# Which row tile's statistics run on ScalarE at the head of an attention kernel

## The chip, the cores and the metric

The kernel runs on one core of one Trainium2 chip. The metric is the device time of one execution in microseconds; lower is better. The kernel before took 1938.25 us, the median of three runs (1937.86 to 1939.1).

## The reference, cut to what matters

A layer norm of x (2048 rows of 640) feeds an attention with 32 heads of width 192 over a cached K and V, and a gated feed-forward of width 1536. The two results are multiplied and added to x. All is in bfloat16.

```python
def reference(A_x, A_k_cache, A_v_cache, A_wq, A_wo, B_x, B_w1, B_w3, B_w2):
    ...
    x = A_x
    xn = _layernorm(x, axis=-1)          # (x - m) / sqrt(v + 1e-5)
    s = _A_ref(xn, A_k_cache, A_v_cache, A_wq, A_wo)
    g = _silu(_B_ref(xn, B_w1, B_w3, B_w2))
    return x + s * g
```

## The kernel before

PE's score and value products make up some 70% of the chain of work that ended last, and PE's other products nearly all of the rest. The change is in what comes first: the layer norm of the first 512 rows (four tiles of 128), which must be ready before PE can turn (transpose) and project them. This beginning of the kernel is called its head below; an attention head is named as such. There are two ways to get a tile's statistics, one on VectorE and one on ScalarE:

```python
    def ln_stats(g, i):                       # VectorE
        ...
        for a in range(nsub):
            nc.vector.bn_stats(out=stats[:, a, :], in_=xr[:, a, :])
        nc.vector.bn_aggr(out=mv[:, i, :], in_=stats[:])
        if i % 2 == 1:                        # the pair is complete: add eps, take the power
            nc.vector.tensor_scalar(out=ve[:, i - 1:i + 1, 0], in0=mv[:, i - 1:i + 1, 1], scalar1=eps, ...)
            ln_rstd(g, i)                     # GpSimd: rstd = ve ** -0.5, for both tiles of the pair

    def ln_stats_act(g, i):                   # ScalarE: mean, then sum of squares about it
        ...
        nc.scalar.activation(out=xns[g, i][:], in_=xi, func=ACT.Identity, scale=1.0 / D, accum_out=mv[:, i, 0:1])
        nc.scalar.activation(out=xns[g, i][:], in_=xi, func=ACT.Square, scale=-1.0, bias=mv[:, i, 0:1], accum_out=ss[:])
        lnorm["ss"] = ss
```

The head then runs:

```python
    def head_start():
        load_x(0, 0, 2)                       # tiles 0 and 1 of x
        load_x(0, 2, 4)                       # tiles 2 and 3
        load_k0(0, nc.sync)
        load_w0()
        turn_over(44)                         # PE: 44 products to keep it busy
        ln_stats(0, 0)
        ln_stats(0, 1)
        ln_stats_act(0, 3)
        load_k0(1, nc.scalar)                 # second half of the first K head
        load_x(1, queue=nc.scalar)
        load_v(0, (0,), nc.scalar)
        ln_stats(0, 2)
        ... # adds of tiles 2 and 3
        ln_rstd(0, 3)
        load_w(1)
        for i in range(4):
            ln_norm(0, i, nc.vector)
        ...
        ln_turn(0, 0, nc.scalar.copy)         # PE transposes of tiles 0 and 1
        turn_k0(pk0, 0, range(4))             # PE transposes of the first half of K
        ln_turn(0, 1, nc.vector.tensor_copy)
        turn_k0(pk1, 1, (0, 1))
        swap_halves(0)                        # DMA: copy with partitions 0-63 and 64-127 exchanged
        ...
        load_v(0, (1,))
        load_x(2)                             # same queue, behind the swap
        project_first()
        ...
        ln_turn_dma(1, 0)                     # transposing loads of the second block's tiles,
        ln_turn_dma(1, 1)                     # same queue, behind load_x(2)
```

After it comes the stream of heads, blocks of 512 rows and pairs of key tiles. Two of its steps: `project(1, 0)`, the first projection that reads the swapped copy (`xnS`), and `project0(1)`, which needs the tiles that `ln_turn_dma` turned.

```python
        if h == 0 and qb == 0 and p == 3:
            project(1, 0)
        if h == 0 and qb + 1 < NQB and p == (5 if qb == 0 else 4):
            project0(qb + 1)
```

Of the kernel before, what the change touches and what calls it, by code (L numbers as in the profile page):

```python
# [9 lines left out]
ALU = mybir.AluOpType  # L10
# [118 lines left out]
def _kernel_impl(  # L129
# [12 lines left out]
    nc = tc.nc  # L142
    _, SQ, D = A_x.shape
    _, H, SK, dh = A_k_cache.shape
# [15 lines left out]
    eps = 1e-5  # L160
# [52 lines left out]
    def load_x(g, t0=0, t1=4, queue=nc.sync):  # L213
        queue.dma_start(out=x_sb[:, 4 * g + t0:4 * g + t1, :],
                          in_=x2[g * 512:(g + 1) * 512, :].rearrange("(p t) d -> p t d", t=4)[:, t0:t1, :])
# [5 lines left out]
    def load_w0():  # L221
        W = wqp.tile([P, 2 * DC, P], BF16, tag="W", name="W")
        nc.gpsimd.dma_start(out=W[:, 0:DC, :], in_=A_wq[:, 0:P].rearrange("(c p) d -> p c d", p=P))
        nc.gpsimd.dma_start(out=W[:, DC:2 * DC, 0:PGW], in_=gate_cols(0).rearrange("(c p) f -> p c f", p=P))
        nc.gpsimd.dma_start(out=W[:, DC:2 * DC, PGW:P], in_=A_wq[:, P:DH].rearrange("(c p) d -> p c d", p=P))
        loads.setdefault(0, {}).update(W=W)

    def load_w(h):

        W = wqp.tile([P, 2 * DC, P], BF16, tag="W", name="W")  # L230
        nc.gpsimd.dma_start(out=W[0:64, :, :], in_=A_wq[:, h * DH:h * DH + P].rearrange("(j p) d -> p j d", p=64))
        if h < 2 * NPIG:
            nc.gpsimd.dma_start(out=W[64:P, :, 0:PGW], in_=gate_cols(h).rearrange("(j p) f -> p j f", p=64))
        else:
            nc.gpsimd.memset(W[64:P, :, 0:PGW], 0.0)
        nc.gpsimd.dma_start(out=W[64:P, :, PGW:P],
                            in_=A_wq[:, h * DH + P:(h + 1) * DH].rearrange("(j p) d -> p j d", p=64))
        loads.setdefault(h, {}).update(W=W)
# [21 lines left out]
    def load_k0(half, queue):  # L260
        if half == 0:
            kn = stp.tile([P, NQT, HG * DH], BF16, tag="ostage", name="kn")
            k0["v"] = kn[:].rearrange("p t c -> p (t c)")[:, 0:NKT * DH].rearrange("p (j c) -> p j c", c=2 * DH)
            loads.setdefault(0, {}).update(KW=kvp.tile([P, 5, HK], BF16, tag="KW", name="KW"))
        queue.dma_start(out=k0["v"][:, half * HP:(half + 1) * HP, :].rearrange("p j c -> p (j c)"),
                          in_=A_k_cache[0, 0, half * HK:(half + 1) * HK, :].rearrange("(p t) d -> p (t d)", p=P))

    def turn_k0(dst, half, sel):
        for a in sel:
            for b in range(HP):  # L270
                nc.tensor.transpose(out=dst[:, a, b * P:(b + 1) * P],  # L271
                                    in_=k0["v"][:, half * HP + b, FIRST[a]:FIRST[a] + P], identity=ident_bf[:])
# [10 lines left out]
    def load_v(h, halves=(0, 1), queue=nc.sync):  # L283


        vt = vts[h % 2]
        for t in halves:
            if h == 0:
                queue.dma_start(out=vt[:, t * NPAIR:(t + 1) * NPAIR, 0:DH],
                                  in_=A_v_cache[0, h, t * HK:(t + 1) * HK, :].rearrange("(i s) d -> i s d", i=P))  # L290
            else:
                nc.sync.dma_start(out=vt[:, :, 0:DH].rearrange("i (p t) d -> i p t d", t=2)[:, :, t, :],
                                  in_=A_v_cache[0, h].rearrange("(p i t) d -> i p t d", i=P, t=2)[:, :, t, :])
        loads.setdefault(h, {}).update(vt=vt)
# [11 lines left out]
    lnorm = {}  # L306

    def ln_stats(g, i):
        if i == 0:
            lnorm[g] = [lnp.tile([P, 4, n], F32, tag=t, name=t)  # L310
                        for t, n in (("mv", nc.vector.BN_AGGR_DIM), ("ve", 1), ("rstd", 1))]
        mv, ve, rstd = lnorm[g]
        stats = lnp.tile([P, nsub, nc.vector.BN_STATS_DIM], F32, tag="stats", name="stats")
        xr = x_sb[:, 4 * g + i, :].rearrange("p (a f) -> p a f", a=nsub)
# [3 lines that stand above are left out]
        if i % 2 == 1:  # L318
            nc.vector.tensor_scalar(out=ve[:, i - 1:i + 1, 0], in0=mv[:, i - 1:i + 1, 1], scalar1=eps, scalar2=None,
                                    op0=ALU.add)  # L320
            ln_rstd(g, i)

    def ln_rstd(g, i):
        mv, ve, rstd = lnorm[g]
        if i % 2 == 1:
            two = slice(i - 1, i + 1)
            nc.gpsimd.tensor_tensor(out=rstd[:, two, 0], in0=ve[:, two, 0], in1=mhalf[:, two], op=ALU.pow)
# [3 lines left out]
    def ln_stats_act(g, i):  # L331


        mv, ve, rstd = lnorm[g]
        ss = lnp.tile([P, 1], F32, tag="ss", name="ss")
        xns[g, i] = xnp.tile([P, D], BF16, tag="xn", name="xn")
        xi = x_sb[:, 4 * g + i, :]
# [4 lines that stand above are left out]
    def ln_norm(g, i, engine):  # L342
        mv, _, rstd = lnorm[g]
        if (g, i) not in xns:
            xns[g, i] = xnp.tile([P, D], BF16, tag="xn", name="xn")
        engine.tensor_scalar(out=xns[g, i][:], in0=x_sb[:, 4 * g + i, :], scalar1=mv[:, i, 0:1], scalar2=rstd[:, i, 0:1],  # L346
                             op0=ALU.subtract, op1=ALU.mult)

    def ln_turn(g, i2, copy):
        pst = ps_st.tile([P, 2, DC, P], BF16, tag="st2", name="pst")  # L350
        for k in range(2):
            xn = xns.pop((g, 2 * i2 + k))
            for c in range(DC):
                nc.tensor.transpose(out=pst[:, k, c, :], in_=xn[:, c * P:(c + 1) * P], identity=ident_bf[:])  # L354
        q0 = (4 * g + 2 * i2) * P
        copy(out=xnT[:, :, q0:q0 + 2 * P].rearrange("p c (k q) -> p k c q", k=2), in_=pst[:])
# [213 lines left out]
    def turn_over(k):  # L570
        for i in range(k):
            nc.tensor.matmul(warm, lhsT=ident_bf[:], rhs=ident_bf[:], start=True, stop=True)

    def head_start():

        load_x(0, 0, 2)
        load_x(0, 2, 4)
        load_k0(0, nc.sync)
        load_w0()
        turn_over(44)  # L580
        ln_stats(0, 0)
        ln_stats(0, 1)
        ln_stats_act(0, 3)
        load_k0(1, nc.scalar)
        load_x(1, queue=nc.scalar)
        load_v(0, (0,), nc.scalar)
        ln_stats(0, 2)
        mv, ve, _ = lnorm[0]
        nc.vector.tensor_scalar(out=ve[:, 2, :], in0=mv[:, 2, 1:2], scalar1=eps, scalar2=None, op0=ALU.add)
        nc.vector.tensor_scalar(out=ve[:, 3, :], in0=lnorm["ss"][:], scalar1=1.0 / D, scalar2=eps,  # L590
                                op0=ALU.mult, op1=ALU.add)
        ln_rstd(0, 3)
        load_w(1)
        for i in range(4):
            ln_norm(0, i, nc.vector)
        pk0 = ps_o.tile([P, 4, 512], BF16, tag="ob0", name="pk0")
        ln_turn(0, 0, nc.scalar.copy)
        turn_k0(pk0, 0, range(4))
        ln_turn(0, 1, nc.vector.tensor_copy)
        turn_k0(pk1, 1, (0, 1))  # L600
        swap_halves(0)
        copy_k0(nc.scalar.copy, pk0, 0, 0)
        copy_k0(nc.scalar.copy, pk0, 0, 1)
        copy_k0(nc.vector.tensor_copy, pk1, 1, 0)
        load_v(0, (1,))
        load_x(2)
        project_first()
        turn_k0(pk1, 1, (2, 3))
        copy_k0(nc.scalar.copy, pk1, 1, 1)
        scores(0)  # L610
        shift_first()
        shift_k0()
        scores(1)
        ln_stats(1, 0)
        ln_stats(1, 1)
        ln_stats(1, 2)
        ln_norm(1, 0, nc.vector)
        ln_norm(1, 1, nc.vector)
        ln_turn_dma(1, 0)
        ln_turn_dma(1, 1)  # L620
        for g in range(3, NQB):
            load_x(g)
        ln_stats(1, 3)

    head_start()

    def finish_block(n):
# [71 lines left out]
    for qb in range(NQB):  # L699
        qs = slice(qb * 512, (qb + 1) * 512)  # L700
        for fl in range(FL2 // P):
            ps = pools[(qb * (FL2 // P) + fl) % 2].tile([P, 1024], F32, tag="st2", name="ps_gu")
            for r, w in enumerate((wrest["w1"], wrest["w3"])):
                for c in range(DC):
# [7 lines left out]
                                           op0=ALU.mult, op1=ALU.mult)  # L712
# [14 lines left out]
    for i in range(NQT):  # L727
# [5 lines left out]
        for b, (c0, c1) in enumerate(DP):  # L733
# [4 lines left out]
                                           in0=t[:, 0:c1 - c0].rearrange("p (a w) -> p a w", w=P), scalar=1.0,  # L738
# [72 lines left out]
```

## Time and profile before

| | before |
|---|---|
| median, three runs | 1938.25 us |
| span of the profiled run | 1936.4 us |
| PE busy | 1926.6 us, 99% |
| granted PE clock | 0.999 |
| VectorE's first statistics to PE's first transpose | 3.58 to 7.60 us |

The table by stretches of the profile of before shows where PE has any idle time (columns: stretch and its length in us; busy us and count for PE, PE's weight loads, VectorE, ScalarE and GpSimd; clock; DMA share; GB/s):

```profile
0.00:10.00 10.00, 6.29 (x86) 6.05 (x87) 5.35 (x20) 4.58 (x7) 6.88 (x14) 1.00 0.76 246
10.00:20.00 10.00, 9.69 (x118) 6.44 (x118) 8.44 (x24) 8.16 (x11) 1.42 (x3) 1.00 1.16 228
20.00:30.00 10.00, 9.87 (x124) 6.18 (x123) 8.11 (x21) 5.21 (x7) 2.69 (x5) 1.00 1.15 208
60.00:120.00 60.00, 60.00 (x928) 40.68 (x924) 21.98 (x31) 41.87 (x44) 12.14 (x21) 1.00 0.40 82
1800.00:1936.00 136.00, 131.18 (x967) 92.50 (x966) 20.50 (x42) 0.00 (x0) 4.84 (x9) 0.99 0.62 118
```

From 60 us on PE is full until its last product ends at 1931.2 us; in the 5.2 us after that the last result is added up and stored, which the change does not reach. So what it can win or lose lies in the beginning. There the DMA engines are busy as well from 10 to 30 us (mean share 1.16 and 1.15; a packet's whole time is counted where it starts, so a share can pass 1).

PE's start of the second block's projection, in its timeline of before:

```profile
24.84 2.32 PE L410 MATMUL ps<-xnT,W 128*128 128x512 bf16 x9
```

The landing records of the trace have the last part of the second transposing load at 24.70 us.

### The profile page before, as it was taken

Reading aid. Unit: us, or ns where it says so; the run is one execution under the profiler, and the core shown is the slowest. Engines: PE = TensorE matmul, PEld = TensorE weight load, DVE = VectorE, ACT = ScalarE, POOL = GpSimd, SP = SyncE. Lnnn points to the kernel's source line nnn. Section 1 sums busy time; section 2 is a strip of 40 time slices with the busy share of each in tenths; the row PEclk is TensorE's granted clock in tenths of the full one; section 3 lists DMA queues with packets and bytes.
Section 4 is the critical chain, followed back from the end, with each engine's and each line's share of the span. In section 5 each row is a group of like instructions: output and inputs, shape, how many; then the busy total and the mean of one; then the engine's idle time right before and its main releaser. Section 6 shows DMA issues by size and latency. Waiting matters only on the chain.

```text
span 1936.4 us, 59669 instructions
## 1 busy us (share of the span) xinstructions
PE 1926.6 (99%) x27273; PEld 1315.6 (68%) x27281; DVE 654.6 (34%) x997; ACT 1180.0 (61%) x1279; POOL 282.5 (15%) x501
## 2 busy tenths in 40 slices
PE   9999999999999999999999999999999999999998
PEld 6666666666666666666666666666666666577776
DVE  7333333333333333333333333333333334521111
ACT  6677676767676767776777777677767677210000
POOL 3111111111111111111111111111111110000000
PEclk9999999999999999999999999999999999999999
DMA  8643433323333434363434343434334220937783
GB/s 181 129 101 67 98 68 86 84 62 88 59 90 61 100 63 97 68 162 69 101 66 100 69 101 69 101 64 101 69 69 96 58 68 2 260 69 137 151 152 62
DMA packets 394643, 178.98 MB, mean 92 GB/s; under 512 B 341616, under 2 KB 382832, under 8 KB 394384
## 3 DMA queue, kind: packets, MB, share of 16 engines
q1 hardware_dynamic: 371136, 125.32, 31.6%
q0 software_dynamic: 19472, 45.71, 10.0%
q8 instruction: 215, 3.52, 0.8%
q10 hardware_dynamic: 3776, 4.06, 0.7%
q14 instruction: 44, 0.36, 0.1%
HBM read 52.82 MB, written 27.79 MB: 42 GB/s over the span
## 4 chain that ended last, share of the span: by engine, by line
PE 99%; DVE 1%; DMA 0%; ACT 0%; issue 0%; DVEq 0%; ACTq 0%
PE obank L519 35%; PE st L487 34%; PE ps L424 14%; PE ps_s L111 11%; PE ps_f L731 3%; PE ps_gu L705 1%; PE st L488 1%; PE ps L410 0%; DVE stats L316 0%; DMA x_all<-in_A_x_dram 0%; PE ps L391 0%; PE pst L354 0%; PE pk L271 0%; DVE xn L346 0%; ACT pT L493 0%
## 5 line engine op out<-in xcount | busy, mean ns | idle before, releaser
L493 ACT ACTIVATE pT<-st 128x1024 bf16<-128x1024 f32 (+1 forms) x1025 | 1046.1, 1021 | 250.2 <-PE st L488 234.0
L519 PEld LDWEIGHTS <-pT 64*128 64x128 bf16 x16384 | 711.3, 94 | 242.3 <-ACT pT L493 0.6
L519 PE MATMUL obank<-vt,pT 64*128 64x193 bf16 x16384 | 849.7, 243 | 0.0
L487 PE MATMUL st<-qC,KW 64*128 64x512 bf16 x2046 | 605.6, 376 | 0.1
L528 DVE COPY osum<-obank 128x772 f32<-128x772 f32 x128 | 123.1, 962 | 787.1 <-PE obank L519 787.1
L488 PE MATMUL st<-qB,KW 64*128 64x512 bf16 x1024 | 385.0, 376 | 0.0
L487 PE MATMUL st<-qA,KW 64*128 64x512 bf16 x1022 | 384.3, 376 | 0.1
L488 PE MATMUL st<-qC,KW 64*128 64x512 bf16 x1022 | 384.3, 376 | 0.0
L488 PE MATMUL st<-qA,KW 64*128 64x512 bf16 x1022 | 384.3, 376 | 0.0
L487 PEld LDWEIGHTS <-KW 64*128 64x128 bf16 x3068 | 278.5, 94 | 153.7 <-issue 2.1
L424 PE MATMUL ps<-xnT,W 64*128 64x512 bf16 x1280 | 297.2, 376 | 0.0
L424 PE MATMUL ps<-xnS,W 64*128 64x512 bf16 x1280 | 296.0, 376 | 0.0
L488 PEld LDWEIGHTS <-KW 64*128 64x128 bf16 x3068 | 278.5, 94 | 0.5
L377 POOL DMA_DIRECT2D qC<-qA x124 | 65.4, 528 | 1283.0 <-DVE rl_all L535 1268.2
L430 ACT CAST qB<-ps 128x512 bf16<-128x512 f32 x131 | 76.7, 585 | 228.2 <-PE ps L424 222.6
L111 PE MATMUL ps_s<-wo_sb,oT 128*128 128x384 bf16 (+3 forms) x1535 | 208.8, 299 | 0.1
L424 PEld LDWEIGHTS <-W 64*128 64x128 bf16 x2560 | 122.9, 94 | 121.4 <-issue 0.2
L111 PEld LDWEIGHTS <-oT 128*128 128x128 bf16 x1536 | 148.4, 98 | 60.4
L529 DVE TENSOR_TENSOR osum<-osum,obank 128x772 f32<-128x772 f32 x128 | 122.7, 959 | 13.4
L536 DVE TENSOR_TENSOR ostage<-osum,rl_all 128x768 bf16<-128x768 f32 x128 | 122.7, 958 | 6.3 <-DMA o_scr<-ostage 1.9
L465 DVE SCALAR_TENSOR_TENSOR hT<-pt,qB 64x512 bf16<-64x512 bf16 x64 | 43.8, 684 | 197.4 <-ACT pt L464 197.4
L429 DVE CAST qA<-ps 128x512 bf16<-128x512 f32 x131 | 90.6, 692 | 25.3 <-PE ps L410 7.2
(84 smaller groups left out, 621.9 us busy)
## 6 DMA issues: line engine op xcount, KB each, us to landing
o_scr<-ostage SPq DMA_DIRECT2D x16, 1536.0 KB, 10.6
vt<-in_A_v_cache_dram SPq DMA_DIRECT2D x63, 384.0 KB, 5.9
qC<-qA POOLq DMA_DIRECT2D x248, 64.0 KB, 1.9
qC<-qB POOLq DMA_DIRECT2D x124, 64.0 KB, 2.3
wo_sb<-in_A_wo_dram POOLq DMA_DIRECT2D x1, 7680.0 KB, 36.1
W<-in_A_wq_dram POOLq DMA_DIRECT2D x32, 160.0 KB, 3.6
W<-in_B_w_dram POOLq DMA_DIRECT2D x32, 80.0 KB, 3.3
W<-in_A_wq_dram POOLq DMA_DIRECT2D x32, 80.0 KB, 3.0
```

What stands on the lines that cost most here:

```text
L111: nc.tensor.matmul(ps[:, 0:w], lhsT=oT[:, k, :], rhs=wo_sb[:, k, c0:c1], start=(k == 0), stop=(k == OC - 1))
L377: nc.gpsimd.dma_start(out=qC[0:64, half, :], in_=qAB[half][64:P, :])
L424: nc.tensor.matmul(ps[:, r * 512:(r + 1) * 512], lhsT=W[rows, j, :], rhs=xs[rows, j // 2, qs], start=(j == 0), stop=(j == 2 * DC - 1))
L429: a = nc.vector.tensor_copy(out=qAB[0][:], in_=ps[:, 0:512])
L430: b = nc.scalar.copy(out=qAB[1][:], in_=ps[:, 512:1024])
L487: nc.tensor.matmul(st2[:, 0:512], lhsT=ka, rhs=qa, start=r == 0 and nr == 3, stop=r == nr - 1)
L488: nc.tensor.matmul(st2[:, 512:1024], lhsT=kb, rhs=qb2, start=r == 0 and nr == 3, stop=r == nr - 1)
L493: nc.scalar.activation(out=pT2[:, c * w:(c + 1) * w], in_=st2[:, c * w:(c + 1) * w], func=ACT.Exp, scale=att_scale)
L519: nc.tensor.matmul(obanks[r][:, j * 256:j * 256 + DH + 1], lhsT=pT2[r * 64:(r + 1) * 64, t * 512 + j * P:t * 512 + (j + 1) * P], rhs=vt[r ...
L528: nc.vector.tensor_copy(out=osum[:], in_=ov[0])
L529: nc.vector.tensor_tensor(out=osum[:], in0=osum[:], in1=ov[1], op=ALU.add)
L536: nc.vector.tensor_tensor(out=ostage[:, qb * 4:qb * 4 + 4, hg * DH:(hg + 1) * DH], in0=osum[:, :, 0:DH], in1=rl.unsqueeze(2).to_broadcast( ...
```

## The change

The intent: the first pair of tiles (0 and 1) should have its powers early, between VectorE's statistics of tiles 2 and 3. So tile 1, of the first half of x, goes to ScalarE in place of tile 3, of the second half.

```diff
         ln_stats(0, 0)
-        ln_stats(0, 1)
-        ln_stats_act(0, 3)
+        ln_stats_act(0, 1)
         load_k0(1, nc.scalar)
         load_x(1, queue=nc.scalar)
         load_v(0, (0,), nc.scalar)
+        mv, ve, _ = lnorm[0]
+        nc.vector.tensor_scalar(out=ve[:, 0, :], in0=mv[:, 0, 1:2], scalar1=eps, scalar2=None, op0=ALU.add)
         ln_stats(0, 2)
-        mv, ve, _ = lnorm[0]
-        nc.vector.tensor_scalar(out=ve[:, 2, :], in0=mv[:, 2, 1:2], scalar1=eps, scalar2=None, op0=ALU.add)
-        nc.vector.tensor_scalar(out=ve[:, 3, :], in0=lnorm["ss"][:], scalar1=1.0 / D, scalar2=eps,
+        nc.vector.tensor_scalar(out=ve[:, 1, :], in0=lnorm["ss"][:], scalar1=1.0 / D, scalar2=eps,
                                 op0=ALU.mult, op1=ALU.add)
-        ln_rstd(0, 3)
+        ln_rstd(0, 1)
+        ln_stats(0, 3)
```

## The prediction

> **What bounds the kernel now.** I read the page first, then the chain of waits for the first 16 us, then each engine's timeline there, then the DMA issues with their landings. The page says who owns the time:
>
> ```profile
> PE 1926.6 (99%) x27273; PEld 1315.6 (68%) x27281; DVE 654.6 (34%) x997; ACT 1180.0 (61%) x1279; POOL 282.5 (15%) x501
> PEclk9999999999999999999999999999999999999999
> PE 99%; DVE 1%; DMA 0%; ACT 0%; issue 0%; DVEq 0%; ACTq 0%
> ```
>
> PE is busy for 99% of a 1936.4 us span at full granted clock, and the chain that ended last is PE's for 99%. The change touches only the layer-norm statistics of the first 512 rows, all of it before 9 us. So it can be worth no more than a piece of PE's idle time at the start. The table by stretches shows how little that is: in the first 60 us PE is busy 55.62 us, idle 4.38, and of that 2.77 us is before the identity exists, which the change does not reach.
>
> The chain of waits (columns: start, length, what) shows who sets PE's start:
>
> ```profile
> 0.75 2.81 DMA x_all<-in_A_x_dram
> 3.58 0.90 DVE stats L316 x2
> 4.50 0.21 DVE mv L317
> 4.71 0.76 DVE stats L316 x2
> 5.50 0.22 DVE mv L317
> 5.74 0.17 DVE ve L319
> 5.91 0.80 DVE stats L316 x2
> 6.73 0.22 DVE mv L317
> 6.97 0.15 DVE ve L589
> 7.13 0.06 DVE ve L590
> 7.19 0.36 DVE xn L346
> 7.60 0.81 PE pst L354 x10
> ```
>
> The reader is to see that from the landing of x at 3.56 to the first transpose at 7.60 VectorE runs without a hole: three tiles' statistics, their small adds, one normalisation. The powers on GpSimd and the fourth tile's statistics on ScalarE are nowhere in it. The timelines of GpSimd and ScalarE say how far off they are:
>
> ```profile
> 4.66 0.74 ACT L338 ACTIVATE xn<-x_all 128x640 bf16<-128x640 bf16 x1 [2.63 <-DMA x_all<-in_A_x_dram]
> 5.53 0.83 ACT L339 ACTIVATE xn<-x_all,mv 128x640 bf16<-128x640 bf16 x1
> 6.00 0.72 POOL L327 TENSOR_TENSOR rstd<-ve,mhalf 128x2 f32<-128x2 f32 x1 [1.58 <-DVE ve L319]
> 7.27 0.83 POOL L327 TENSOR_TENSOR rstd<-ve,mhalf 128x2 f32<-128x2 f32 x1 [0.55 <-DVE ve L590]
> 8.13 0.90 DVE L346 TENSOR_SCALAR xn<-x_all,mv,rstd 128x640 bf16<-128x640 bf16 x2 [0.23 <-POOL rstd L327]
> ```
>
> The first pair's power ends at 6.72, VectorE gets round to the normalisation that needs it at 7.11: 0.39 us of slack. The second pair's power does hold VectorE, for 0.23 us, before row tile 2 is normalised; but PE takes that tile's transposes only at 9.14, after 16 transposes of K, so that wait too costs nothing.
>
> PE then has one more hold that matters. At 18.84 it begins the first two-part projection, which reads the half-swapped copy of the normalised rows:
>
> ```profile
> 18.84 0.38 PE L424 MATMUL ps<-xnT,W 64*128 64x512 bf16 x1
> 19.05 0.39 PE L424 MATMUL ps<-xnS,W 64*128 64x512 bf16 x2
> ```
>
> In the later projections (46.39, 61.43) the two rows of the array start together; here the second starts 0.21 us late. The swap copies were issued at 10.81 and 11.57, with 6.6 and 7.4 us to landing, so the second lands at 11.57 + 7.4 = 18.97. PE waits for it. At 24.84 PE starts the next full projection some 0.25 us late in the same way: the two transposing loads issued from 17.98 on land around 24.7.
>
> **What the Trainium skill says.** "VectorE: DVE Perf Modes", section "The DRAIN you can't avoid": a next vector operation does not start until the pipe is empty, and a semaphore costs nothing extra. The trace half agrees: an aggregate is followed 0.13 us later (4.50 to 4.63) by an operation that does not read it, but 0.24 us later by one that does (5.50 to 5.74, 6.73 to 6.97). So the order of VectorE's small operations is worth about a tenth of a microsecond per place, and I count those. "DMA: Bandwidth & Descriptors", section "Issuing engines are not separate DMA queues": transfers of all issuing engines run on the same 16 DMA engines and interleave. The trace agrees: the mean share is 0.92 to 1.45 in nearly every half microsecond from 7 to 19 us, with loads of three issuers in flight. The section "Queues, rings and completion order" there adds that each engine takes turns between the queues it has work for, and that a transfer is split over up to 16 of them; I use it below for the slowest engine.
>
> **The change part by part.**
> Removed: VectorE's statistics of tile 1, ScalarE's of tile 3. Added: VectorE's of tile 3, ScalarE's of tile 1. The comparison of instruction order says that PE, ScalarE, GpSimd and the DMA issues keep their sequence and counts; on VectorE the same 13 operations stand in another order. So the sum of work is unchanged, and only gaps can differ.
>
> VectorE, step by step from 3.58, with the durations above. Tile 0: two statistics, aggregate at 4.50. Its add reads the aggregate: 4.50 + 0.24 = 4.74. The next statistics follow a small add by 0.08 (5.74 to 5.82): 4.82. This is tile 2, of the second half of x. That half releases ScalarE now at 4.66, so it is there by about 4.64: 0.18 us to spare. Aggregate 0.91 later, 5.73. The next add reads ScalarE's sum and not the aggregate, so it comes 0.13 later: 5.86, if the sum is ready. Statistics of tile 3 at 5.94, aggregate 6.85, the pair add 7.09 (0.24), first normalisation 7.15 to 7.17 (0.06 to 0.08). Now it is 7.11. So the path to PE's first transpose gets longer by about 0.05 us, since there are now three small adds between the statistics in place of two there and one pair at the end.
>
> ScalarE: tile 1 is in the first half of x, so it starts at about 3.58 in place of 4.66, 1.08 us sooner. From 4.66 to the last accumulator read (6.26 + 0.19) it now needs 1.79 us; the sum is ready at 5.37, half a microsecond before VectorE asks at 5.86.
>
> GpSimd: the first power starts 0.22 to 0.26 after its add, 6.10, and ends about 6.83: 0.34 us before VectorE's 7.17. The second starts at 7.09 + 0.26 = 7.35 and ends at about 8.15; tile 2's normalisation follows at 8.18 in place of 8.13. PE needs that tile only at about 9.19.
>
> DMA issues: the three loads on ScalarE's queue (second half of the first K head, second block of x, first half of V) follow ScalarE's statistics. They were issued from 5.53 and will be from about 4.45. Now the DMA share drops to 0.60 and 0.88 in the half microseconds from 6.0 and 6.5; that hole will be filled, about 0.26 us of DMA time on the mean engine. None of the three is waited for now: the second half of K lands at 5.53 + 3.6 = 9.13 and is used at 9.70, the block of x lands at 10.8 and is used at 14.29, V at 12.7 and is used at 14.74.
>
> On PE: +0.05 us from 7.60 on, through 18.84. At 18.84 stands the wait for the swap, of 0.21 us. If the swap lands when it does now, the 0.05 us disappear in that wait and everything after it is as before. If the filled hole lets it land earlier, PE gains up to 0.2 us there. The swap's landing is set by the slowest of 16 DMA engines; its backlog did not have the hole, I think, since the last parts of the first K load were still arriving around 7.7 (1.68 + 6.0). So I take most of this gain as not coming. Sum: +0.05 - 0.05, and about -0.05 as an expectation of the gain: 1938.25 becomes 1938.2.
>
> **The rivals.**
> 1. The DMA stream shifts forward. For it: the hole at 6 to 7 us, and shares about full until 19, so a lead given there could be carried to the swap (18.97) and to the transposing loads (24.7). Then PE gains 0.2 us at 18.84 and up to 0.25 at 24.84: about 1937.8. Against: the slowest engine decides, and the transposing loads also wait for VectorE's normalisation at 17.56.
> 2. A new wait takes the place of an old slack. Tile 2's statistics now stand 0.18 us behind their DMA where they stood 1.2 us behind it, and the first half of K (landing at 7.7, used at 8.25) must share the engines with loads issued 1.08 us sooner. If either comes late by 0.2 us over its slack, PE starts 0.2 us later and part of it is eaten again at 18.84: about 1938.3 to 1938.5.
> 3. A real gain at the head, as the change intends: the pair's power early, so that the first normalisation starts sooner. Against: the normalisation comes behind three tiles' statistics on VectorE both before and after, and the power has 0.39 us of slack already. This would need VectorE to be waiting before 7.11, and it isn't. I give it little.
>
> **Range and chances.** All rivals lie within 0.5 us, 0.03% of the time. The three runs of before spread over 1.24 us (1937.86 to 1939.1), more than any effect here, so the range is that noise on a median plus the rivals: 1937.0 to 1939.4, centred on 1938.2. A change of 2% would be 39 us, nine times all the idle time that PE has in its first 60 us. Chance of within 2%: 0.99.
>
> **What would show it.** In the chain of waits after the change: DVE statistics from 3.58 on, an add at 4.74, the first transpose at about 7.65. ScalarE's Identity pass at about 3.6, its sum by 5.4, its DMA issues from about 4.45. First power from 6.1, second from 7.35. A VectorE wait on x near 4.8 would speak for the second rival; PE's two array rows starting together at the projection near 18.9 would speak for the first; PE's first transpose before 7.5 would break my reading of the head. A median outside the range would mean that the change reached the steady state, for which I see no way.

## The result, and the profile after

The changed kernel took 1939.35 us, the median of six runs (1937.9 to 1940.47); the kernel before took 1938.24 us in six runs (1937.86 to 1939.1). The ratio is 1.0005 with a 95% interval of 0.9992 to 1.0018: the same. A ratio here is the mean time of one kernel's fast runs over that of the other's of the same rounds, so it is not quite the ratio of the medians.

The profiled execution of the changed kernel took 1938.36 us, span 1936.6. Its chain of waits at the head (start, length, what):

```profile
0.75 3.00 DMA x_all<-in_A_x_dram
3.77 0.90 DVE stats L316 x2
4.70 0.22 DVE mv L317
4.94 0.15 DVE ve L587
5.09 0.81 DVE stats L316 x2
5.92 0.21 DVE mv L317
6.13 0.02 DVE ve L589
6.14 0.80 DVE stats L316 x2
6.97 0.22 DVE mv L317
7.21 0.17 DVE ve L319
7.38 0.36 DVE xn L346
7.79 0.81 PE pst L354 x10
```

Everything is 0.19 us later than before, and so is its beginning: x landed at 3.75 in place of 3.56. From the first statistics to PE's first transpose it is 7.79 - 3.77 = 4.02 us, and before 7.60 - 3.58 = 4.02. The head did not change in length.

ScalarE and GpSimd moved as intended (timelines of the changed kernel):

```profile
3.77 0.74 ACT L338 ACTIVATE xn<-x_all 128x640 bf16<-128x640 bf16 x1 [1.74 <-DMA x_all<-in_A_x_dram]
4.64 0.39 ACTq L265 DMA_DIRECT2D kn<-in_A_k_cache_dram  x1
6.25 0.72 POOL L327 TENSOR_TENSOR rstd<-ve,mhalf 128x2 f32<-128x2 f32 x1 [1.83 <-DVE ve L589]
7.46 0.82 POOL L327 TENSOR_TENSOR rstd<-ve,mhalf 128x2 f32<-128x2 f32 x1 [0.50 <-DVE ve L319]
```

ScalarE starts with the first half of x, and its loads go out at 4.64 in place of 5.53. The first power ends at 6.97, while VectorE gets to the first normalisation at 7.29: it was not what VectorE waited for before, and it is not now.

PE's two later holds, in the timeline of the changed kernel:

```profile
19.03 0.38 PE L424 MATMUL ps<-xnT,W 64*128 64x512 bf16 x1
19.27 0.39 PE L424 MATMUL ps<-xnS,W 64*128 64x512 bf16 x2
25.02 2.32 PE L410 MATMUL ps<-xnT,W 128*128 128x512 bf16 x10
```

Both are still there: 0.24 us for the swap (0.21 before), and the second block's projection at 25.02 (24.84). The two traces can be laid over each other by ScalarE's 1025 exponentials. Counted from the first statistics, the changed kernel's come at the same times to within 0.01 us at 14 us and from 28 us on to the last one at 1642 us.

So the profiles show a change worth nothing. But the other runs of the changed kernel reach 1940.47 us, 1.4 us above the highest of before. Is that the change, or the execution? And why can a kernel with 99% PE vary by a microsecond?

### The profile page after: what moved, and what is told of

It is laid out like the page before. It is cut to its first block, busy times and chain, and to the rows that moved or that the text cites. A ratio compares the mean times of both kernels' runs of the same rounds, so it can differ in the third digit from the quotient of the medians.

```text
span 1936.6 us, 59677 instructions
## 1 busy us (share of the span) xinstructions
PE 1927.5 (100%) x27281; PEld 1316.0 (68%) x27281; DVE 654.4 (34%) x997; ACT 1181.2 (61%) x1279; POOL 282.5 (15%) x501
## 4 chain that ended last, share of the span: by engine, by line
PE 99%; DVE 1%; DMA 0%; ACT 0%; issue 0%; DVEq 0%; ACTq 0%
PE obank L519 35%; PE st L487 34%; PE ps L424 14%; PE ps_s L111 11%; PE ps_f L731 3%; PE ps_gu L705 1%; PE st L488 1%; PE ps L410 0%; DVE stats L316 0%; DMA x_all<-in_A_x_dram 0%; PE ps L391 0%; PE pst L354 0%; PE pk L271 0%; DVE xn L346 0%; ACT pT L493 0%; DVE osum L529 0%
## 5 line engine op out<-in xcount | busy, mean ns | idle before, releaser
L111 PE MATMUL ps_s<-wo_sb,oT 128*128 128x256 bf16 (+3 forms) x1536 | 208.8, 299 | 0.0
```

The source lines that it names most:

```text
L111: nc.tensor.matmul(ps[:, 0:w], lhsT=oT[:, k, :], rhs=wo_sb[:, k, c0:c1], start=(k == 0), stop=(k == OC - 1))
```

## The experiments

Three theories were open. Theory 1: the change is neutral, and the times vary with landings of DMAs that the change doesn't touch. Theory 2: the loads on ScalarE's queue, now issued 0.9 us sooner, hold up the slowest DMA engines, and PE waits in some executions. Theory 3: the head's length matters, but the waits near 19 and 25 us swallow what it gains or loses. Twelve kernels ran; each was timed in five rounds against the kernel before. All gave right results.

### The kernel before against itself

No edit but an empty line at the end.

> The kernel before once more, under another name, against itself: the noise floor. All theories: ratio 1.0000, times between about 1937.8 and 1939.2 us. If its own runs also reach 1940 us, the spread of the changed kernel's runs (1937.9 to 1940.5) is noise of the execution; if they stay under 1939.2, that spread belongs to the change. In its profile, from the first statistics of VectorE to PE's first transpose: 4.02 us, as before (3.58 to 7.60).

Measured: 1938.76 us (1937.78 to 1938.9), before in the same rounds 1938.28 (1937.88 to 1939.81); ratio 1.0000, interval 0.9986 to 1.0013. The noise floor for five runs is thus about 0.5 us in the median, and the kernel before alone reaches 1939.81. By the rule set above, the renamed copy's own runs, all under 1939.2, speak for the spread of the changed kernel being its own; the run at 1939.81, of the same program, speaks against it. So the rule decided nothing. The profile (a run of 1938.9 us) shows one of its sources, in PE's timeline:

```profile
7.79 0.81 PE L354 MATMUL pst<-ident_bf,xn 128*128 128x128 bf16 x10 [0.22 <-DVE xn L346]
19.03 0.38 PE L424 MATMUL ps<-xnT,W 64*128 64x512 bf16 x1
20.00 0.39 PE L424 MATMUL ps<-xnS,W 64*128 64x512 bf16 x2 [0.59 <-DMA xnS<-xnT]
25.73 1.89 PE L410 MATMUL ps<-xnT,W 128*128 128x512 bf16 x7
```

The head again takes 4.02 us (3.77 to 7.79). But here the last of the swap's 16 parts landed at 19.95, against 19.01 in the first profile, though it was issued only 0.18 us later (11.75 and 11.57); the next-to-last landed at 18.45, against 18.25. One slow part of one transfer cost PE 0.76 us. The transposing loads stand behind in the same queue and land at 25.59 in place of 24.70, and the projection starts at 25.73. So 0.7 us of difference between two executions of one kernel come from one late part, a straggler.

### The changed kernel again

> The changed kernel again. Theory 1 (no effect; all that differs is when the first block of x lands): median within 0.3 us of the kernel before in the same rounds, first statistics to first transpose 4.02 us again. Theory 2 (the loads on ScalarE's queue, issued 0.9 to 1.1 us sooner, hold up the slowest DMA engines, and in some executions PE waits for the second half of K): median 0.5 to 1.5 us over the kernel before, single runs at 1939.5 us and above, and the second half of K landing at 9.5 us or later in the profile, against 9.1 before.

Measured: 1939.01 us (1937.87 to 1939.13), ratio 1.0002, interval 0.9988 to 1.0015. Its profile (a run of 1938.03 us) has the head at 4.03 us (3.64 to 7.67), the second half of K at 8.89 us, sooner than before (9.11), and the projection at 24.74. The signs disagree. The profile speaks for theory 1, and no run reaches the 1939.5 us of theory 2; but the median, 0.73 us over that of before, lies in theory 2's range, though the mean is only 0.02% higher. K's landing alone tells little: it was 9.71 us in the first profile of the changed kernel, as theory 2 wanted, but 9.79 in the renamed copy of the old one.

### The exchange alone, with the powers late

The tiles exchanged as in the change, but the first pair's adds and power behind all of VectorE's statistics:

```diff
+        ln_stats(0, 2)
+        ... bn_stats and bn_aggr of tile 3 ...
         nc.vector.tensor_scalar(out=ve[:, 0, :], ...)
-        ln_stats(0, 2)
         nc.vector.tensor_scalar(out=ve[:, 1, :], in0=lnorm["ss"][:], ...)
         ln_rstd(0, 1)
-        ln_stats(0, 3)
+        ... add of tiles 2 and 3, ln_rstd(0, 3) ...
```

> The exchange of tiles alone: tile 1 on ScalarE, but the first pair's adds and power behind all three of VectorE's statistics and ahead of the second pair's. Expected: last aggregate 3.02 us after the first statistics, first power from about 3.4 to 4.15 us after them, first normalisation at 4.2 in place of 3.53, so PE's first transpose some 0.65 us later. If the wait for the half-swapped rows near 19 us absorbs what comes late (the swap's landing set by the DMA backlog), the exponentials after 20 us are 0.4 to 0.45 us later than before; if the swap lands a fixed time after its issue, the full 0.65 us, and the time is 0.65 us longer.

Measured: 1939.11 us (1938.42 to 1939.6), ratio 1.0004, interval 0.9990 to 1.0017. PE's timeline:

```profile
8.36 0.45 PE L354 MATMUL pst<-ident_bf,xn 128*128 128x128 bf16 x5 [1.30 <-DVE xn L346]
19.60 0.38 PE L424 MATMUL ps<-xnT,W 64*128 64x512 bf16 x1
19.60 0.59 PE L424 MATMUL ps<-xnS,W 64*128 64x512 bf16 x2
25.25 2.33 PE L410 MATMUL ps<-xnT,W 128*128 128x512 bf16 x9
```

The first statistics were at 3.81, so the head is 8.36 - 3.81 = 4.55 us, 0.53 longer than 4.02. Now the power is on the path (idle 1.30 us before the transposes). This is what the second half of the change, "powers between the statistics", is worth: with the exchange it is needed to lose nothing. But of the 0.53 us only 0.33 are left in the exponentials at 22 us and 0.20 from 28 us on. At 19.60 PE finds the swap landed (18.75), so the 0.2 us wait is gone; at 25 us it finds the transposing loads landed (24.61), and the rest of the slack is gone. The swap was issued 0.75 us later than before and landed 0.26 us sooner. One pair of profiles can owe that to a straggler, but the eighth of the 16 parts of the second copy landed at 17.25 us in both. So within these 0.75 us the landing did not follow the issue. That fits a landing set by the DMA engines' backlog; no run measures the backlog by itself. A good part of what the head loses is swallowed, as theory 3 says.

### ScalarE's loads held back

```diff
         ln_stats_act(0, 1)
+        nc.scalar.activation(out=hT[:, 0, 0:D], in_=x_sb[:, 1, :], func=ACT.Square)
         load_k0(1, nc.scalar)
```

> The changed kernel with one spare pass of ScalarE over tile 1 (its output is overwritten later) ahead of the three loads on its queue, so that they are issued at about 5.3 us, near the 5.53 of before, in place of 4.6. VectorE's order is the changed one. Theory 1: the same time as the changed kernel and the kernel before within 0.3 us. Theory 2: the extra time of the changed kernel goes away, the second half of K lands near 9.1 us again, and no run is above 1939.2 us.

Measured: 1938.16 us (1937.8 to 1939.56, two of the five above 1939), ratio 1.0001, interval 0.9988 to 1.0015. The experiment failed in what it set out to do: ScalarE's timeline has the loads issued at 4.60 and the spare pass at 5.42. The pass took its place in ScalarE's work without holding the issues behind it. So this is another head like the changed one, with a length of 7.75 - 3.73 = 4.02 us, and its times tell nothing of theory 2.

### The first swapped projection moved later

Into the kernel before, and into the changed one:

```diff
-        if h == 0 and qb == 0 and p == 3:
+        if h == 0 and qb == 0 and p == 5:
             project(1, 0)
-        if h == 0 and qb + 1 < NQB and p == (5 if qb == 0 else 4):
+        if h == 0 and qb + 1 < NQB and p == (6 if qb == 0 else 4):
             project0(qb + 1)
 ...
         if qb == 0 and p == 3:
             ln_stats(2, 0)
+        if qb == 0 and p == 4:
             ln_turn(1, 1, nc.vector.tensor_copy)
             swap_halves(1)
```

> The kernel before, with the first projection that reads the half-swapped rows moved two steps of the stream later (step 5 in place of 3), the second block's transposes one step later and its projection from step 5 to 6. If the wait for the slowest part of the swap near 19 us (0.2 us in the profile of before, 0.9 us in the run of the same kernel under another name) makes the spread of the times, the wait is gone here: PE's two array rows start together in that projection, the median is 0.3 to 0.6 us lower (about 1937.8), and the highest of the runs is under 1938.8. If the spread comes from elsewhere, it stays at 1.2 us or more.

> The same move in the changed kernel. With the absorbing wait gone, what the change does at the head shows in full. Theory 1 (the head takes the same time, -0.01 us by the profiles): the same median as the other kernel with the move, within 0.3 us. Theory 2 (ScalarE's earlier loads cost in some executions): median 0.5 us or more above it. The prediction's step of 0.05 us more at the head is too small for the times; in the profile it would be 4.07 us from first statistics to first transpose, against 4.02.

Measured: 1940.51 us (1940.21 to 1941.76), ratio 1.0010, interval 0.9997 to 1.0024, and 1940.42 us (1939.97 to 1942.48), ratio 1.0011, interval 0.9997 to 1.0024. A miss: both medians rose by 2.2 to 2.3 us, and the spread did not shrink. PE's timeline of the first (its slowest run, 1941.76 us) shows why:

```profile
10.77 0.62 PE L271 MATMUL pk<-ident_bf,kn 128*128 128x128 bf16 x8 [0.77 <-DMA kn<-in_A_k_cache_dram]
28.65 2.33 PE L410 MATMUL ps<-xnT,W 128*128 128x512 bf16 x10 [0.83 <-DVE qA L429]
31.76 0.39 PE L487 MATMUL st<-qA,KW 64*128 64x512 bf16 x1 [0.79 <-DVE qA L429]
```

With the projections one step apart, PE waits for VectorE's casts of their results. These stand behind the third block's statistics, which wait for x until 23.2 us. A third wait, of 0.68 us, stands at 26.32, for VectorE's copy of the turned rows. The move traded one DMA wait for three VectorE waits. The pair still tells two things. The two heads again differ by nothing in the medians (0.09 us). And the first line shows the kernel with the head of *before* waiting 0.77 us and more for the second half of K, which landed at 10.72: this wait, which theory 2 wanted for the changed kernel, is found with the old head as well. In the profile of the other kernel (again its slowest run) K landed at 10.40, and the first V, also one of ScalarE's loads, at 17.15 held PE for 1.56 us.

### Two tiles on ScalarE

Tiles 1 and 3 on ScalarE, VectorE left with 0 and 2; alone, and with the moved projection:

```diff
         ln_stats_act(0, 1)
+        ss1 = lnorm["ss"]
         load_k0(1, nc.scalar)
+        ln_stats_act(0, 3)
 ...
-        ln_stats(0, 3)
+        ... add of tile 2, ln_norm of tiles 0 and 1, add of tile 3 from ScalarE's sum, ln_rstd(0, 3) ...
```

> Tiles 1 and 3 both on ScalarE, VectorE left with tiles 0 and 2, the first two normalisations before the last add. If VectorE's chain of three statistics sets PE's first transpose, it comes 0.3 to 0.45 us sooner (3.6 to 3.7 us after the first statistics). But the second pair's power waits for ScalarE's second tile, some 0.5 us later than before, so PE waits there: the first exponential moves by -0.1 to +0.2 us after the first statistics, and the time within 0.3 us of before. If PE's order at the head doesn't matter that way, the whole 0.3 us reaches the exponentials.

> Both of the last two: two tiles on ScalarE and the projection two steps later. Expected: the time of the kernel before with the moved projection, plus or minus 0.2 us, with PE's first transpose 0.3 to 0.45 us sooner; a gain of more than 0.3 us over that kernel would say that the head was the bound and that the wait at 19 us had hidden it.

Measured: 1938.94 us (1938.56 to 1942.65), ratio 1.0006, interval 0.9993 to 1.0020, and 1941.72 us (1941.43 to 1942.52), ratio 1.0017, interval 1.0003 to 1.0031. The head of the first is 7.32 - 3.71 = 3.61 us, 0.41 shorter: VectorE's chain of three statistics did set PE's start. The first exponential gains 0.09 us of it, since PE then waits for the second pair's normalisation; K had landed at 9.20, before its turn at 9.74. And none of that arrives in the profile:

```profile
7.32 0.81 PE L354 MATMUL pst<-ident_bf,xn 128*128 128x128 bf16 x10 [0.53 <-DVE xn L346]
18.89 0.38 PE L424 MATMUL ps<-xnT,W 64*128 64x512 bf16 x1
20.23 0.39 PE L424 MATMUL ps<-xnS,W 64*128 64x512 bf16 x2 [0.97 <-DMA xnS<-xnT]
25.99 2.32 PE L410 MATMUL ps<-xnT,W 128*128 128x512 bf16 x10
```

The swap's last part landed at 20.19, the transposing loads at 25.85; whether this straggler comes from the new head or from the execution is not shown. This head works no better for the second pair, so it was no candidate for a faster kernel; the combined kernel was 1.2 us slower than the one with the moved projection and the old head, where 0.2 us to either side was expected. Its profile has one wait more, of 0.78 us for the second half of V at 21.80; whether every run has it is not shown.

### The transposing loads taken off the path

By now PE's start of the second block's projection had followed the last landing of the transposing loads by 0.13 or 0.14 us in six of seven profiles, whatever the head did; the late power's was the exception, where PE came after them. The hold itself is short. From the start of PE's last product before it to the start of this projection it is 0.18 us in the late power and in the four kernels below, where nothing holds PE, and 0.26 to 0.35 us in the six (0.32 before): the loads hold PE for 0.08 to 0.17 us. So the last four kernels turn the two tiles on PE:

```diff
-        ln_turn_dma(1, 0)
-        ln_turn_dma(1, 1)
 ...
+        if qb == 0 and p == 2:
+            ln_turn(1, 0, nc.scalar.copy)
         if qb == 0 and p == 3:
             ln_stats(2, 0)
```

That was put into the kernel before, into the changed one, into the changed one with tile 0's add moved down next to tile 1's, and into the late power.

> The kernel before, with the first two row tiles of the second block turned on PE (ten transposes and a copy on ScalarE, behind step 2) in place of the two transposing loads. In six profiles so far (before, changed and four others with the same order at 25 us) PE's start of the next projection followed the landing of these loads by 0.13 us, whatever the head did. If that pins everything after it: the wait is gone here (0.3 us in the profile of before, more where the loads land late), ten transposes cost 0.56 to 0.66 us, so the median is within 0.4 us of before, and the spread of the five runs falls under 1 us. If the spread comes from elsewhere it stays at 1.2 us or more.

> The same in the changed kernel. If the change is neutral at the head, as its profiles say (-0.01 us from the first statistics on), the median is within 0.2 us of the kernel before with the same move; if ScalarE's earlier loads cost something, it is 0.5 us or more above it.

> The same move and the changed head, with tile 0's add put next to tile 1's, behind the second tile's aggregate, so that no small add reads the aggregate just ahead of it but the last pair's. By the gaps in the profiles (0.24 us behind an aggregate that is read at once, 0.13 otherwise) VectorE's chain is 0.1 us shorter, so first statistics to first transpose 3.9 us in place of 4.02, unless the second half of x, needed 0.1 us sooner, is late. In the times at most 0.1 us, within the noise.

> The same move and the late power, which made PE's first transpose 0.53 us later and the rest only 0.2 us later from 28 us on. If the transposing loads absorbed the difference, it is not absorbed here: the exponentials after 28 us come 0.4 to 0.53 us later than in the kernel before with this move, counted from the first statistics. If the swap near 19 us absorbs too, 0.2 us less.

Measured (before: 1938.24 us, 1937.88 to 1939.2):

| head, with tiles turned on PE | median (range) us | ratio to before |
|---|---|---|
| as before | 1938.86 (1938.83 to 1939.13) | 1.0003 |
| changed | 1939.25 (1938.64 to 1939.9) | 1.0004 |
| changed, adds together | 1938.77 (1938.59 to 1939.68) | 1.0004 |
| late power | 1939.35 (1939.17 to 1940.76) | 1.0007 |

Each interval includes 1 and reaches 0.13% to either side. The spread fell to 0.3 us with the old head, as expected, but stayed at 1.1 to 1.6 us with the others, so the loads are not its only source. Two expectations on the times were missed: the old head with the move is 0.62 us over the kernel before, where at most 0.4 was expected, and the changed head is 0.39 us over the old one, between the 0.2 of theory 1 and the 0.5 of theory 2.

The profiles give the clean answer, because nothing is swallowed here any more. From the first statistics to PE's projection at 25 us:

| head, with tiles turned on PE | to first transpose | to projection |
|---|---|---|
| changed, adds together | 7.62 - 3.78 = 3.84 | 25.29 - 3.78 = 21.51 |
| as before | 7.95 - 3.93 = 4.02 | 25.92 - 3.93 = 21.99 |
| changed | 7.85 - 3.84 = 4.01 | 25.89 - 3.84 = 22.05 |
| late power | 8.29 - 3.74 = 4.55 | 25.95 - 3.74 = 22.21 |

```profile
7.62 0.81 PE L354 MATMUL pst<-ident_bf,xn 128*128 128x128 bf16 x10 [0.49 <-DVE xn L346]
25.29 2.33 PE L410 MATMUL ps<-xnT,W 128*128 128x512 bf16 x9
```

```profile
8.29 0.81 PE L354 MATMUL pst<-ident_bf,xn 128*128 128x128 bf16 x10 [1.48 <-DVE xn L346]
25.95 1.68 PE L410 MATMUL ps<-xnT,W 128*128 128x512 bf16 x6
```

The late power (second timeline) comes 0.71 us later at the first transpose than the adds together (first timeline), and 0.70 us later at the projection: the head passes on whole. The exponentials say the same of all four: against the kernel before, and counted from the first statistics, each kernel loses the same 0.44 us between its exponentials near 14 us and those near 29 us (from -0.17 to 0.27, 0.31 to 0.75, 0.37 to 0.81 and 0.53 to 0.97 us, in the table's order). The comparison that had been announced, late power against the old head, gives only 22.21 - 21.99 = 0.22 us in place of 0.4 to 0.53. The old head and the changed one have one accident each beside the 0.18 and 0.17 us of their heads, seen in PE's timelines, first of the old head, then of the changed one:

```profile
7.95 1.12 PE L354 MATMUL pst<-ident_bf,xn 128*128 128x128 bf16 x10 [0.30 <-DVE xn L346]
8.90 1.06 PE L271 MATMUL pk<-ident_bf,kn 128*128 128x128 bf16 x16
```

```profile
7.85 0.81 PE L354 MATMUL pst<-ident_bf,xn 128*128 128x128 bf16 x10 [0.78 <-DVE xn L346]
9.39 0.72 PE L354 MATMUL pst<-ident_bf,xn 128*128 128x128 bf16 x10
10.31 0.62 PE L271 MATMUL pk<-ident_bf,kn 128*128 128x128 bf16 x8 [0.20 <-DMA kn<-in_A_k_cache_dram]
```

With the old head the first ten transposes took 1.12 us in place of 0.81 (the next group began 0.95 us after them and not 0.65): PE lost 0.3 us because it was still at a slow rate. The trace shows it: its record of the full clock begins at 8.79 us, and until then PE's products started 107 ns apart, afterwards 56 ns. (The clock column of the stretches shows 1.00 all the same: it takes time without a record for full speed.) In the first profile of before it begins at 5.45 us, and the 44 products ahead of the transposes took 3.89 us in place of 4.87. The Trainium skill ("TensorE: Matmul & The Clock Gate", "What's actually happening") says that the activity window behind the clock runs freely, so the point where it warms up varies by 500 ns either way. That it varies is so here, but by more: in the fourteen profiles the full clock begins between 5.45 and 8.79 us, while the first of the 44 products starts at 2.77 or 2.78 in all of them. With the changed head the second half of K landed at 10.26, and its transposes began at 10.31 where 9.39 + 0.56 = 9.95 was due (0.56 us being the step from 9.14 to 9.70 in the first profile): 0.36 us. With these, 0.18 + 0.30 and 0.17 + 0.36 make the 0.48 and 0.54 us that the projections differ from 21.51.

### All profiles together

The three with the moved projection are left out, since their projection L410 stands elsewhere.

| kernel | first statistics | transposing loads landed | projection L410 | span | span - L410 |
|---|---|---|---|---|---|
| before | 3.58 | 24.70 | 24.84 | 1936.4 | 1911.6 |
| changed | 3.77 | 24.89 | 25.02 | 1936.6 | 1911.6 |
| before, renamed | 3.77 | 25.59 | 25.73 | 1937.1 | 1911.4 |
| changed, again | 3.64 | 24.61 | 24.74 | 1936.2 | 1911.5 |
| late power | 3.81 | 24.61 | 25.25 | 1936.6 | 1911.4 |
| spare pass | 3.73 | 24.84 | 24.98 | 1936.4 | 1911.4 |
| two tiles on ScalarE | 3.71 | 25.85 | 25.99 | 1937.5 | 1911.5 |
| turned on PE, as before | 3.93 | none | 25.92 | 1937.4 | 1911.5 |
| turned on PE, changed | 3.84 | none | 25.89 | 1937.4 | 1911.5 |
| turned on PE, adds together | 3.78 | none | 25.29 | 1936.8 | 1911.5 |
| turned on PE, late power | 3.74 | none | 25.95 | 1937.5 | 1911.5 |

Everything after the projection takes 1911.4 to 1911.6 us in each. So all but 0.2 of the 1.3 us by which these spans differ lie in the first 26 us. There, in the kernel as it stands, they lie in when the first x landed and in when the queue of swap, x and transposing loads had. In the changed kernel the landing was 0.19 us later than before, and the span is 0.2 us longer.

## Why the prediction was right or wrong

It said 1938.2 us, range 1937.0 to 1939.4, and "the same". The measured 1939.35 is inside by 0.05 us, and three of the six runs lay above the range: that the number held is in part luck. The mechanism, a VectorE chain that the change reorders and doesn't shorten, is what the profiles show. 0.05% is far inside the 2%.

- *VectorE sets the first transpose, and the power has slack.* Right. Two tiles on ScalarE shortened the head by 0.41 us, and a power taken late lengthened it by 0.53. Rival 3, a real gain from the early power, is refuted: VectorE never waited for the first pair's power in before.
- *The head gets 0.05 us longer.* Wrong in its size: 0.00 (4.02 and 4.02). Counted from the first statistics, each VectorE instruction came within 0.02 us of its predicted place up to the add from ScalarE's sum. The term that was mis-sized is the step from that add to the next statistics: taken as 0.08 us, from an add that reads the aggregate just before it, it was 0.02 (6.04 to 6.06 in VectorE's timeline).
- *ScalarE starts with the first half of x, its sum half a microsecond early, its loads 0.9 to 1.1 us sooner.* Right: 3.77, and issued at 4.64. The sum's last read ends at 5.37 + 0.19 = 5.56, 0.48 us ahead of VectorE's add at 6.04.
- *The hole in the DMA stream is filled, but the swap lands no sooner, since the slowest engine had no hole.* Borne out for the result. The share from 6.0 to 6.5 us rose from 0.60 to 0.92, the eighth of the second swap's 16 parts landed at 17.19 against 17.25, and the last one later (19.23 against 19.01). Rival 1 did not come, nor did rival 2: the second half of x landed at 4.54, and VectorE came to it at 5.01; the first half of K landed at 7.38, and PE came to it at 8.44. That the slowest engine had no hole is argued; the records do not name the engine.
- *What the head loses disappears in the wait at 18.84.* There was nothing to lose here, but the late power shows the step at work, and shows that a second wait, which the prediction named at 24.84 and then left out of its sum, swallows as well: 0.53 us became 0.33 and 0.20. It took that second wait for 0.25 us; by PE's steps above it is 0.14.
- *The range is the noise of three runs plus the rivals.* This was too narrow. Three runs of 1.24 us spread were taken for the whole noise; single runs of the changed kernel went to 1940.47, and one execution of the kernel before to 1939.81. One source was in the profile that I had read: a wait for the last of 16 parts of a DMA, on the path. The late clock and the late K of the last experiment are two others.

What stays open: the kernel before had 33 runs beside the renamed copy's, median 1938.24, four above 1939 us; the changed kernel had 11, median 1939.07, seven above 1939. So the times lean to a real effect. No profile shows its cause. Both profiled executions of the changed kernel were among its fast ones, and the waits on K that theory 2 asked for were found with the old head too. Nor do the landings differ: over the profiles with the old statistics (four) and with the exchanged tiles (eight), the second half of K landed on average at 9.64 and 9.60 us, and the swap's last part at 19.48 and 19.52. The experiment that should have held the loads back didn't hold them. So an effect of some half a microsecond (0.03%), from the earlier loads or from something else, is neither shown nor excluded; the intervals of both comparisons include no effect.

No version beat both kernels. Adds together has the shortest head of those that cost nothing elsewhere (3.84 us), but it was timed only with the tiles turned on PE, which costs 0.5 to 0.6 us; on its own it was not run, and by the landings above its 0.18 us would mostly be swallowed.

## What to carry to other kernels

When a step off the bound is moved, follow PE to the *last* wait that the change's effect must pass, not the first: here a head that lost 0.53 us made the rest only 0.20 us later, and one that won 0.41 us brought PE to the projection at 25 us no sooner in its one profile, since a DMA queue had not landed. Compare two traces from a common event (the first landing), and find the point after which everything takes the same time; it separates the change from the noise far below what timings can. But one profile is one execution: what happens only in some of them, as the slower runs of the changed kernel may, it can miss. And where the path waits for a DMA under a heavy DMA load, expect the time to vary by the slowest of its 16 parts (here by 0.7 us), and set the range by that.

## What the Trainium skill lacked or had wrong

- "DMA: Bandwidth & Descriptors" gives no figure for how the last of the 16 parts scatters from execution to execution under load: the same 320 KB copy of the swap took 7.4 us from issue to landing in one profile of the kernel before and 8.2 in the other, with the last part 0.76 and 1.50 us behind the next-to-last (19.01 and 18.25; 19.95 and 18.45).
- "TensorE: Matmul & The Clock Gate", "What's actually happening", has the clock's warm-up vary by 500 ns either way. In the fourteen profiles the full clock began between 5.45 and 8.79 us, a spread of 3.3 us.
- "VectorE: DVE Perf Modes", "The DRAIN you can't avoid", says from a test with copies that a semaphore between two operations costs nothing extra, and has no figure for small operations. An add that reads the aggregate just ahead of it started 0.24 us after the aggregate did (6.97 to 7.21 in the changed kernel), just after its end; an add that does not read it started 0.12 us after it (5.92 to 6.04), before its record ended at 6.13. No run separates a semaphore's cost from this earlier start.
- No page, "Perfetto Trace Analysis" included, says of a DMA issue on ScalarE's queue whether it waits for activations queued before it. In the run with the spare pass it did not: issued at 4.60, with the pass at 5.42.
